# A planner's rule for blocks sent over GpSimd: which buffer the test for a free one looks at, in an induced-attention and feed-forward kernel

## The chip, the core and the metric

The kernel runs on one core of a Trainium2 chip. The metric is the device time of one execution in microseconds (us); of the kernel before it is the median of three runs. The engines are PE (TensorE, the matrix multiplier), DVE (VectorE), ACT (ScalarE), POOL (GpSimd) and SP, which issues most transfers. PEld is PE's loading of weights.

## What is computed

```python
def _attn_ref(x, inducing):                # x: 4 x 12480 x 128, inducing: 32 x 128
    def mab(q, kv):
        s = scale * (q @ kv.transpose(0, 2, 1))
        s = s - s.max(-1, keepdims=True)
        a = np.exp(s)
        a /= a.sum(-1, keepdims=True) + 1e-09
        return a @ kv
    h = mab(I, x)                          # 32 rows for each of the 4 batches
    return mab(x, h)
def _moe_ref(x, w_in, w_out):              # w_in: 128 x 2048, w_out: 2048 x 128
    h = x @ w_in
    g = np.maximum(0.01 * h, h)
    return g @ w_out
```

Each batch is read twice: a first pass makes the 32 rows h, a second lets every token attend to them, and the result goes through a feed-forward layer with a leaky activation.

## The kernel before

**Tiles.** The 49,920 tokens are cut into about 98 tiles of 512 (`tiles`; two are made of remainders and have 384). The 2048 hidden features are NF = 16 blocks of 128. A tile and a block (t, f) make one unit of work: a first product (the folded weights `hw` by the attention rows A, three quarter matmuls of 32 rows), an activation, a split of the activated block into a high part `ghi` and a low part `glo`, and second products that add w_hi·ghi, w_lo·ghi and w_hi·glo to the tile's output. The 0.01 part is linear and goes through a small matrix of its own.

**The two ways of a split.** The near way: ACT writes `ghi` from the PSUM bank (L1078, `high`), DVE writes `glo` from the same bank and `ghi` (L1081, `low`); the bank comes free after DVE. The far way: ACT writes the whole activated block to a buffer `g` (L1078 too), the bank comes free at once, and POOL makes `ghi` (a cast, L1352) and `glo` (a subtraction, L1354) from `g`. There are two buffers `g`, used in turn. In the first two tiles the same far way stands at L1050 to L1059.

**The first two tiles** (`rounds`, QUICK = 2). PE runs whole 128-row second products (L1122) in an order written out by hand. `split_first` chooses the way. `others(u)` is called after each of the 32 units u and advances the background work by a step each: conversion of the weights (`late`, whose last add on POOL is L225, with the split into w_hi and w_lo at L276 and L278), scores and values of the next batch, stores, `stacking`, and `seconds`, the second attention (`second`: scores L388, maximum L875, subtraction L879, exponent L887, sum L893, scaling L901, transpose L912). For the first group of the first batch `second` is told to use DVE in place of POOL.

**The rest** is laid out by a list planner (`turn_over`) that keeps a clock for each engine, takes the work that can start first, and emits it; the engines then run what was emitted in that order. PE runs as four row groups of 32 rows (`quarter`, L1091), a block's second products in all four, and up to GB = 10 blocks are under way. When a first product is done, `relu(i, ...)` decides between the two ways by these lines:

```python
left = far_ends[-2] if len(far_ends) > 1 else 0.0
wanted = now[0] + (i - turn_of[0]) * SLOT - EARLY
if far_open[0] < 2 and left <= start and far <= wanted:
```

`start` is when ACT could begin, `far_ends` the planned ends on POOL of the blocks whose POOL work is already laid out, `far_open` the number handed over whose POOL work is not yet laid out. After a tile's last block, ACT copies two of its four partial sums (L1380), DVE adds the other two (L1386), POOL joins them (L1397) and DVE transposes the result for the store (L1145). Work that doesn't run in four row groups, which is the scores (L388), maxima (L422), values (L559) and a few small products, waits until the planner gathers it (`clustered`), and then interrupts the quarter matmuls. `first_scores` lets group n of the next batch begin no earlier than n · PACE after that batch's begin, by the planner's clock.

Of the kernel before, what the change touches and what calls it, by code (L numbers as in the profile page):

```python
# [19 lines left out]
def induced_attention_then_leaky_ffn(  # L20
# [20 lines left out]
    nc = tc.nc  # L41
# [4 lines left out]
    NF = DFF // P  # L46
# [21 lines left out]
    PE, ACT, DVE, POOL, SP = "PE", "ACT", "DVE", "POOL", "SP"  # L68
# [14 lines left out]
    QUICK = 2  # L83
# [6 lines left out]
    SIGNAL, TO_ARRAY, TO_POOL = 35.0, 55.0, 70.0  # L90
# [3 lines left out]
    RELU, LOW, COPIED, ADDED, BLOCKS = 599.0, 690.0, 587.0, 691.0, 702.0  # L94
    FAR_HIGH, FAR_LOW, FAR_SUM = 613.0, 1297.0, 1297.0
    EARLY, PREFER, YIELDING, PATIENCE = 250.0, 0.0, 200.0, 6000.0
    IDLE, HURRY, APART, TAIL, WAITING, SOON = 600.0, 3000.0, 60000.0, 5000.0, 3000.0, 3000.0
    NEAR, BANKS, AT_ONCE, BEHIND = 3, 1, 2000.0, 1200.0
    LINEAR = NF - 3
    BEGUN = 3  # L100
    AHEAD = 100.0
    PACE, STOCK = 37000.0, 4
    debt = [0]

    const = ctx.enter_context(tc.tile_pool(name="const", bufs=1))
# [27 lines left out]
    clock = {ACT: 0.0, DVE: 0.0, POOL: 0.0, SP: 0.0}  # L133
# [4 lines left out]
    def spent(engine, ns, *after):  # L138
        if not timing[0]:
            return 0.0  # L140
        signal = TO_POOL if engine == POOL else SIGNAL
        clock[engine] = max([clock[engine], now[0], *(a + signal for a in after)]) + ns
        return clock[engine]
# [15 lines left out]
    def new(engine, at=0.0):  # L159
        if quads[0]:  # L160
            yield engine, at

    def until(test, engine=None):
        while not test():
            yield (engine, now[0] + 300.0) if quads[0] else None

    def aux_ps(name):
        return bank("aux")
# [681 lines left out]
    def second(b, g, eng=None):  # L850
        eng = eng or nc.gpsimd
        assert coming[0] == (b, g)
        yield from until(lambda: g == RG or sum(q != RG for _, q in aT) < (STOCK if quads[0] else 4))
        if (b, g) != (0, 0):
            yield from new(PE, landed.get((b, "h"), 0.0))
        hT = hw[b][0]
        _, J, K = GROUPS[g]
        rows_, w = 32 * J, 32 * K
        sp = aux_ps("s2_ps")
        for j in range(J):  # L860
            columns_product(sp, hT[:, :M], b, g, j)
        at = on_array("c", 875.0 if g != RG else 120.0, landed.get((b, "h"), 0.0), taken[0])
        del xT[b, g]
        coming.pop(0)
        ring.discard((b, g))
        yield from new(DVE, at)
        y = sb.tile([P, 16, M], F32, tag="y", name="y", bufs=1)
        yv = y[:rows_, :K, :]
        nc.vector.transpose(yv.rearrange("p k m -> p (k m)"), sp[:rows_, :w])
        at = spent(DVE, BLOCKS, at)  # L870
        done(sp, at)
        yield from old(HEAVY)
        yield from new(DVE, at)
        mx = sb.tile([P, 16], F32, tag="mx", name="mx")
        nc.vector.tensor_reduce(out=mx[:rows_, :K], in_=yv, op=ALU.max, axis=AX.X)  # L875
        at = spent(DVE, 680.0, at)
        yield from old(HEAVY)
        yield from new(POOL, at)
        eng.tensor_tensor(  # L879
            out=yv, in0=yv, in1=mx[:rows_, :K].unsqueeze(2).broadcast_to([rows_, K, M]),  # L880
            op=ALU.subtract,
        )
        at = spent(POOL, 1050.0, at)
        yield from old()
        yield from old()
        yield from new(ACT, at)
        nc.scalar.activation(yv, yv, AF.Exp, scale=SCALE)  # L887
        at = spent(ACT, 635.0, at)
        yield from old()
        yield from new(DVE, at)  # L890
        sm = sb.tile([P, 16], F32, tag="sm", name="sm")
        smv = sm[:rows_, :K]
        nc.vector.tensor_reduce(out=smv, in_=yv, op=ALU.add, axis=AX.X)  # L893
        at = spent(DVE, 680.0, at)
        yield from new(DVE, at)
        nc.vector.tensor_scalar_add(smv, smv, 1e-9)
        nc.vector.reciprocal(smv, smv)
        at = spent(DVE, 430.0)
        yield from old(HEAVY)
        yield from new(POOL, at)  # L900
        eng.tensor_tensor(  # L901
            out=yv, in0=yv, in1=smv.unsqueeze(2).broadcast_to([rows_, K, M]), op=ALU.mult
        )
        at = spent(POOL, 1050.0, at)
        yield from old()
        yield from old()
        yield from new(DVE, at)
        if g == RG:
            t = sb.tile([P, w], F32, tag="aTr", name="aTr", bufs=2)
        else:  # L910
            t = sb.tile([P, w], F32, tag="aT", name="aT", bufs=4)
        nc.vector.transpose(t[:rows_, :], yv.rearrange("p k m -> p (k m)"))  # L912
        aT[b, g] = t
        landed[b, g, "aT"] = spent(DVE, BLOCKS, at)
        yield from old(HEAVY)
# [122 lines left out]
        (t, f0) for f0 in range(0, NF, TURN) for t in range(QUICK)  # L1038
    ]

    high_of, low_of = {}, {}

    def split_first(ph, t, f, at):

        _, n = spans(t)
        ghi = sb.tile([P, TOK], F32R, tag="ghi", name="ghi", bufs=GB)
        glo = sb.tile([P, TOK], F32R, tag="glo", name="glo", bufs=GB)
        live[t, f] = (ghi, glo)
        if max(clock[POOL], at + RELU) + FAR_HIGH + FAR_LOW < max(clock[DVE], at + RELU) + LOW + BEHIND:
            g = sb.tile([P, TOK], F32, tag="g", name="g", bufs=2)  # L1050
            high(ph, g, n)
            at = spent(ACT, RELU, at)
            done(ph, at)
            nc.gpsimd.tensor_copy(ghi[:, :n], g[:, :n])
            high_of[t, f] = spent(POOL, FAR_HIGH, at)
            nc.gpsimd.tensor_tensor(  # L1056
                out=glo[:, :n], in0=g[:, :n], in1=ghi[:, :n].bitcast(F32), op=ALU.subtract
            )
            low_of[t, f] = spent(POOL, FAR_LOW)  # L1059
            return  # L1060
        high(ph, ghi, n)
        high_of[t, f] = at = spent(ACT, RELU, at)
        low(ph, ghi, glo, n)
        low_of[t, f] = at = spent(DVE, LOW, at)
        done(ph, at)
# [143 lines left out]
    with tc.manual_schedule():  # L1209
# [40 lines left out]
        def others(u):  # L1250
            debt[0] = max(0, debt[0] - 1)
            if u % 2 == 0:
                step(late)
            step(splits)
            step(weights)
            step(linear)
            if not debt[0] or u < (QUICK + 1) * NF:
                step(stores)
            step(stacking)
            if u % 2 or u < NF - 4 if u < QUICK * NF else not debt[0]:  # L1260
                step(seconds)
            if u >= due[0] and not debt[0]:
                due[0] = u + 2
                step(scores)
            if (u >= due[1] or any(b not in known for b in hw)) and not debt[0]:
                due[1] = u + 2
                if values and not (linear or weights):
                    step(values)
            follow()
# [14 lines left out]
        u = 0  # L1284
        for i, (t, f0) in enumerate(rounds):
            if 0 < i < len(rounds) - 1:
                first_round(*rounds[i + 1])
            for f in range(f0, f0 + TURN):
# [10 lines left out]
                if f == NF - 1:  # L1299
                    at = linear_part(t)  # L1300
# [24 lines left out]
        for t, parts in enumerate(tiles):  # L1325
            for b, g, _ in parts:
                tile_of.setdefault((b, g), t)
        far_ends, far_open, gathering, gang = [], [0], [0], []

        def add(engine, ready, ns, emit, allowed=None, ahead=0.0):  # L1330
            jobs[engine].append((ready, ns, emit, allowed, ahead))
# [4 lines left out]
        def relu(i, ph, ready):  # L1336
            t, f = work[i]
            _, n = spans(t)
            ghi, glo = live[t, f]
            start = max(clock[ACT], ready + SIGNAL)  # L1340
            far = max(clock[POOL], start + RELU) + backlog(POOL) + FAR_HIGH + FAR_LOW
            left = far_ends[-2] if len(far_ends) > 1 else 0.0
            wanted = now[0] + (i - turn_of[0]) * SLOT - EARLY
            if far_open[0] < 2 and left <= start and far <= wanted:
                g = sb.tile([P, TOK], F32, tag="g", name="g", bufs=2)
                high(ph, g, n)
                at = spent(ACT, RELU, ready)
                done(ph, at)
                far_open[0] += 1

                def on_pool():
                    nc.gpsimd.tensor_copy(ghi[:, :n], g[:, :n])  # L1352
                    high_at[i] = spent(POOL, FAR_HIGH, at)
                    nc.gpsimd.tensor_tensor(  # L1354
                        out=glo[:, :n], in0=g[:, :n], in1=ghi[:, :n].bitcast(F32), op=ALU.subtract
                    )
                    low_at[i] = spent(POOL, FAR_LOW)
                    far_ends.append(low_at[i])
                    far_open[0] -= 1

                add(POOL, at, FAR_HIGH + FAR_LOW, on_pool)
                return
            high(ph, ghi, n)
            high_at[i] = at = spent(ACT, RELU, ready)

            def rest():
                low(ph, ghi, glo, n)
                low_at[i] = spent(DVE, LOW, at)
                done(ph, low_at[i])

            add(DVE, at, LOW, rest)
# [240 lines left out]
        t = NT - 1  # L1612
# [48 lines left out]
```

## Time and profile before

| what | value |
|---|---|
| median of the runs | 1562.48 us (1561.61 to 1563.14, 3 runs) |
| the profiled execution | 1562.13 us |
| its span, from first to last instruction | 1560.3 us |
| PE busy | 1542.2 us (99%) |
| POOL busy | 1369.8 us (88%) |
| ACT busy | 1070.8 us (69%) |
| DVE busy | 1020.9 us (65%) |
| mean DMA rate | 82 GB/s |

The profiled execution is 1.8 us longer than its span, and 0.35 us under the median. A busy PE is not a PE at its peak: its matmuls overlap, so the time lost on it is seen in the number of matmuls in a stretch, and in the idle time before weight loads.

### The profile page before, as it was taken

What the parts mean: (1) busy time and instruction counts of PE and PEld (TensorE: products, weight loads), DVE (VectorE), ACT (ScalarE), POOL (GpSimd) and SP (SyncE); (2) the same over time, 40 slices, a digit from 0 to 9 for tenths busy, and PEclk for the clock granted to TensorE, in tenths of its full rate; (3) what the DMA queues carried; (4) which work ended last, traced back from release to release, by engine and by line L of the source; (5) the groups of instructions that cost most, each with busy time, mean ns of one, the idle gap of its engine ahead of it and who ended that gap; (6) DMA issues with size and microseconds to landing.
All of it is one profiled execution on the core that took longest, in us unless ns stands there. A gap on an engine that the chain in (4) does not pass through costs nothing.

```text
span 1560.3 us, 60204 instructions
## 1 busy us (share of the span) xinstructions
PE 1542.2 (99%) x25045; PEld 1353.0 (87%) x25045; DVE 1020.9 (65%) x1809; ACT 1070.8 (69%) x1956; POOL 1369.8 (88%) x1439
## 2 busy tenths in 40 slices
PE   8999999999999999999999999999999999999998
PEld 5578898888888798999998898989988998998896
DVE  7866667656766775666777675665565656575654
ACT  6566666666766676677676676777777777777774
POOL 1589999999999799899978989989999899959997
PEclk9999999999999999999999999999999999999999
DMA  7166454444455432354446433322222223223221
GB/s 273 17 134 110 102 104 95 97 85 93 84 107 112 99 62 66 81 100 91 92 92 131 103 76 68 63 57 56 57 56 58 55 57 63 47 55 63 55 56 24
DMA packets 400705, 128.50 MB, mean 82 GB/s; under 512 B 373136, under 2 KB 375600, under 8 KB 400432
## 3 DMA queue, kind: packets, MB, share of 16 engines
q1 hardware_dynamic: 399328, 124.50, 38.5%
q8 instruction: 197, 3.23, 0.9%
q14 instruction: 76, 0.62, 0.1%
q10 hardware_dynamic: 1104, 0.15, 0.1%
HBM read 48.94 MB, written 25.56 MB: 48 GB/s over the span
## 4 chain that ended last, share of the span: by engine, by line
PE 91%; POOL 4%; issue 2%; ACT 1%; DVE 1%; DMA 1%; SPq 1%; POOLq 0%; ACTq 0%; DVEq 0%
PE bank L1091 83%; PE bank L388 3%; POOL glo L1354 2%; PE bank L559 2%; PE bank L1122 1%; POOL ghi L1352 1%; DMA xr<-in_x_dram 1%; PE bank L708 1%; DVE glo L1081 0%; PE bank L422 0%; ACT ghi L1078 0%; SPq L373 0%; ACT g L1078 0%; POOL glo L1056 0%; PE bank L1132 0%
## 5 line engine op out<-in xcount | busy, mean ns | idle before, releaser
L1091 PE MATMUL bank<-ghi,w_hi 32*128 32x512 f32 (+1 forms) x6080 | 1251.4, 392 | 1.3 <-ACT g L1078 1.1
L1091 PE MATMUL bank<-glo,w_hi 32*128 32x512 f32 (+1 forms) x6080 | 1250.6, 391 | 0.1
L1091 PE MATMUL bank<-ghi,w_lo 32*128 32x512 f32 (+1 forms) x6080 | 1248.3, 390 | 0.0
L1091 PE MATMUL bank<-A,hwhi 32*128 32x512 f32 (+1 forms) x3394 | 1052.2, 389 | 1.6 <-DVE glo L1081 0.6
L1081 DVE SCALAR_TENSOR_TENSOR glo<-bank,ghi 128x512 fp32r<-128x512 f32 (+1 forms) x946 | 630.9, 683 | 367.5 <-ACT ghi L1078 351.2
L1091 PEld LDWEIGHTS bank<-ghi,w_hi 32*128 32x128 f32 x6080 | 822.5, 183 | 37.6 <-ACT g L1078 7.4
L1091 PEld LDWEIGHTS bank<-glo,w_hi 32*128 32x128 f32 x6080 | 825.6, 183 | 25.1 <-POOL glo L1354 1.4
L1091 PEld LDWEIGHTS bank<-ghi,w_lo 32*128 32x128 f32 x6080 | 822.7, 183 | 24.7 <-issue 3.9
L1354 POOL TENSOR_TENSOR glo<-g,ghi 128x512 fp32r<-128x512 f32 (+1 forms) x611 | 790.0, 1293 | 48.9
L1078 ACT ACTIVATE ghi<-bank 128x512 fp32r<-128x512 f32 (+1 forms) x946 | 553.7, 598 | 138.8 <-PE bank L1091 116.1
L1091 PE MATMUL bank<-A,hwlo 32*128 32x512 f32 (+1 forms) x1697 | 612.0, 386 | 0.0
L1091 PEld LDWEIGHTS bank<-A,hwhi 32*128 32x128 f32 x3394 | 568.4, 183 | 31.5 <-DVE glo L1081 5.9
L1078 ACT ACTIVATE g<-bank 128x512 f32<-128x512 f32 (+1 forms) x622 | 371.9, 598 | 275.1 <-PE bank L1091 166.4
L1352 POOL CAST ghi<-g 128x512 fp32r<-128x512 f32 (+1 forms) x611 | 374.9, 614 | 44.6 <-ACT g L1078 35.7
L1091 PEld LDWEIGHTS bank<-A,hwlo 32*128 32x128 f32 x1697 | 297.8, 183 | 5.2 <-issue 0.8
L1386 DVE TENSOR_TENSOR part<-bank,part 128x512 f32<-128x512 f32 (+1 forms) x190 | 129.8, 686 | 97.6 <-ACT part L1380 47.8
L1397 POOL TENSOR_TENSOR part<-part 128x512 f32<-128x512 f32 (+1 forms) x95 | 122.7, 1292 | 15.8 <-DVE part L1386 15.7
L1380 ACT COPY part<-bank 128x512 f32<-128x512 f32 (+1 forms) x190 | 110.6, 587 | 15.0 <-PE bank L1091 12.3
L1145 DVE STREAM_TRANSPOSE osb<-part 128x512 f32<-128x512 f32 (+1 forms) x95 | 66.5, 700 | 9.0 <-POOL part L1397 7.7
L515 DVE STREAM_TRANSPOSE xT<-xc 128x512 f32<-128x512 f32 x72 | 46.4, 683 | 0.0
L448 ACT ACTIVATE e<-e,nm 128x512 f32<-128x512 f32 (+1 forms) x28 | 18.7, 669 | 24.6 <-DVE least L436 21.4
L879 POOL TENSOR_TENSOR y<-y,mx 128x512 f32<-128x512 f32 (+1 forms) x27 | 25.4, 941 | 9.0 <-DVE mx L875 8.6
(122 smaller groups left out, 658.3 us busy)
## 6 DMA issues: line engine op xcount, KB each, us to landing
A<-both SPq DMA_DIRECT2D x376, 128.0 KB, 2.4
xr<-in_x_dram SPq DMA_DIRECT2D x96, 256.0 KB, 4.8
out_dram<-osb SPq DMA_DIRECT2D x382, 64.0 KB, 2.2
xc<-in_x_dram SPq DMA_DIRECT2D x288, 64.0 KB, 2.8
raw<-in_moe_w_in_dram SPq DMA_DIRECT2D x4, 512.0 KB, 6.6
raw<-in_moe_w_out_dram SPq DMA_DIRECT2D x4, 512.0 KB, 8.4
A<-both SPq DMA_DIRECT2D x48, 16.0 KB, 1.8
out_dram<-osb SPq DMA_DIRECT2D x48, 8.0 KB, 1.8
```

What stands on the lines that cost most here:

```text
L388: nc.tensor.matmul(dst, lhsT, rhs, start=True, stop=True)
L515: nc.vector.transpose(t[:, j, :], blk.rearrange("p n c -> p (n c)"))
L559: nc.tensor.matmul(hp[32 * k : 32 * k + 32, :C], ay[:rows_, 4 * q + k, :], xb[:rows_, k, :], start=(q == 0), stop=(4 * q + 4 >= K), tile_p ...
L1078: nc.scalar.activation(ghi[:, :n], ph[:, :n], AF.Relu)
L1081: nc.vector.scalar_tensor_tensor(out=glo[:, :n], in0=ph[:, :n], scalar=0.0, in1=ghi[:, :n].bitcast(F32), op0=ALU.max, op1=ALU.subtract,)
L1091: nc.tensor.matmul(dst, w[32 * r : 32 * r + 32], x[32 * r : 32 * r + 32], start=start, stop=stop, tile_position=(32 * r, 0),)
L1145: nc.vector.transpose(osb[:, :n], total[:, :n])
L1352: nc.gpsimd.tensor_copy(ghi[:, :n], g[:, :n])
L1354: nc.gpsimd.tensor_tensor(out=glo[:, :n], in0=g[:, :n], in1=ghi[:, :n].bitcast(F32), op=ALU.subtract)
L1380: nc.scalar.copy(part[:, :n], po[:, :n])
L1386: nc.vector.tensor_tensor(out=part[:, :n], in0=po[:, :n], in1=part[:, :n], op=ALU.add)
L1397: nc.gpsimd.tensor_tensor(out=total[:, :n], in0=total[:, :n], in1=part[:, :n], op=ALU.add)
```

## The change

It alters five places of the planner; no operation on data is changed.

```diff
-    PACE, STOCK = 37000.0, 4
+    PACE, STOCK = 39000.0, 4
...
-        at = spent(POOL, 1050.0, at)
+        at = spent(*((POOL, 1050.0) if eng is nc.gpsimd else (DVE, 690.0)), at)
...
-        at = spent(POOL, 1050.0, at)
+        at = spent(*((POOL, 1050.0) if eng is nc.gpsimd else (DVE, 690.0)), at)
...
-    high_of, low_of = {}, {}
+    high_of, low_of, far_ends = {}, {}, []
...
-        if max(clock[POOL], at + RELU) + FAR_HIGH + FAR_LOW < max(clock[DVE], at + RELU) + LOW + BEHIND:
+        start = max(clock[ACT], at + SIGNAL)
+        if far_ends[-2:-1] <= [start] and max(clock[POOL], start + RELU) + FAR_HIGH + FAR_LOW < (
+            max(clock[DVE], start + RELU) + LOW + BEHIND
+        ):
...
             low_of[t, f] = spent(POOL, FAR_LOW)
+            far_ends.append(low_of[t, f])
             return
...
-            if u % 2 or u < NF - 4 if u < QUICK * NF else not debt[0]:
+            if u % 2 or u < NF + 4 if u < QUICK * NF else not debt[0]:
                 step(seconds)
...
-        far_ends, far_open, gathering, gang = [], [0], [0], []
+        far_open, gathering, gang = [0], [0], []
...
-            left = far_ends[-2] if len(far_ends) > 1 else 0.0
+            left = far_ends[far_open[0] - 2] if far_open[0] < 2 <= len(far_ends) + far_open[0] else 0.0
```

In `relu`, with one block handed over and not yet laid out, the next `g` is the buffer of the last block laid out, so the test now looks at `far_ends[-1]`, where it looked at `far_ends[-2]`. `split_first` gets a test for a free `g`, and counts from ACT's clock. `second` books the two steps that run on DVE on DVE's clock. `seconds` is advanced at every unit up to u = 19 (it was 11) and at every other one after. PACE goes from 37 to 39 us.

The number of instructions hardly changes: PE has 24,324 matmuls in both programs, and three blocks of 512 columns go from the far way to the near (613 to 610 far, 923 to 926 near, the 384-column ones the same). Their order changes from the middle of the first two tiles to the end. Three places follow; line numbers of the change are 4 higher than before from the relu rule on (L1078 is L1082, L1091 is L1095, L1380 is L1384), and 3 higher in `split_first` (L1054 is L1057, L1056 is L1059).

ACT, at the end of a tile some 456 us into the trace, around the eighth copy of attention rows (`both`); `g` is a block that goes over POOL. Before:

```order
L1078 ACTIVATE g<-bank_67 128x512
L1078 ACTIVATE ghi<-bank_70 128x512
L1078 ACTIVATE g<-bank_65 128x512
L1078 ACTIVATE ghi<-bank_71 128x512
L1078 ACTIVATE g<-bank_67 128x512
L1078 ACTIVATE ghi<-bank_65 128x512
L1078 ACTIVATE g<-bank_70 128x512
L932 CAST both<-aT 128x512
L1380 COPY part<-bank_66 128x512
L1380 COPY part<-bank_64 128x512
```

and now:

```order
L1082 ACTIVATE ghi<-bank_71 128x512
L1082 ACTIVATE ghi<-bank_67 128x512
L1082 ACTIVATE g<-bank_65 128x512
L448 ACTIVATE e,zg<-e,nm 128x512
L455 ACTIVATE al<-nm 128x1
L1082 ACTIVATE g<-bank_71 128x512
L1384 COPY part<-bank_69 128x512
L932 CAST both<-aT 128x512
L1082 ACTIVATE ghi<-bank_65 128x512
L1384 COPY part<-bank_70 128x512
```

Four blocks in seven went to `g` ahead of the copies, with the copies behind them; now two do in the same stretch, and the copies stand among the blocks.

PE, in the first pass over batch 2, around the values of one group (`ay`) and the scores of others (`xT`); each run of rows other than L1091 ends the four row groups for a while. Before, four such runs some 100 rows or fewer apart:

```order
L1091 MATMUL bank_64<-ghi,w_lo 128x512
L422 MATMUL bank_66<-rd,e_74 128x4
L1091 MATMUL bank_65<-ghi,w_hi 128x512
...
L388 MATMUL bank_71<-xT,hT 32x512 x4
...
L388 MATMUL bank_67<-xT,indT 32x512 x4
...
L559 MATMUL bank_65<-xr,ay 32x128 x16
```

and now, at the place nearest to it:

```order
L1095 MATMUL bank_65<-A_9771,hwhi 128x512
L388 MATMUL bank_66<-xT,hT 32x512 x4
L388 MATMUL bank_69<-xT,indT 32x512 x4
L422 MATMUL bank_64<-rd,e_74 128x4
L559 MATMUL bank_66<-xr,ay 32x128 x16
L1095 MATMUL bank_70<-glo,w_hi 128x512
```

The same work stands in one run. Between the first two tiles and the last one, 42 such runs are left of 46.

POOL, at the end of the first two tiles: the last conversion of weights (L225), the split of the last w_out quarter (L278, `w_lo`), and the second attention (`y`). Before:

```order
L225 TENSOR_TENSOR wraw<-cv_a,cv_t 128x512
L879 TENSOR_TENSOR y<-y,mx 128x512
L278 TENSOR_TENSOR w_lo<-wraw,w_hi 128x512
L1054 CAST ghi<-g 128x512
L1056 TENSOR_TENSOR glo<-g,ghi 128x512
L901 TENSOR_TENSOR y<-y,sm 128x512
```

and now:

```order
L225 TENSOR_TENSOR wraw<-cv_a,cv_t 128x512
L901 TENSOR_TENSOR y<-y,sm 128x512
L1057 CAST ghi<-g 128x512
L1059 TENSOR_TENSOR glo<-g,ghi 128x512
L278 TENSOR_TENSOR w_lo<-wraw,w_hi 128x512
L1057 CAST ghi<-g 128x512
```

The subtraction L879 went ahead of L225, and a scaling and a whole far block went ahead of L278.

## Rows read from the trace of the kernel before

**Rows 1.** The page: busy time of the engines, and PE's granted clock by slices.

```profile
PE 1542.2 (99%) x25045; PEld 1353.0 (87%) x25045; DVE 1020.9 (65%) x1809; ACT 1070.8 (69%) x1956; POOL 1369.8 (88%) x1439
...
PEclk9999999999999999999999999999999999999999
```

**Rows 2.** Windows, quarter matmuls alone (L1091): length, PE busy (count), PEld busy (count), clock, DMA.

```profile
90.00:530.00 440.00, 406.42 (x6654) 358.23 (x6657) 1.00 0.51 102
530.00:960.00 430.00, 400.43 (x6814) 368.77 (x6810) 1.00 0.44 89
960.00:1541.00 581.00, 572.93 (x9750) 528.30 (x9742) 1.00 0.27 55
```

**Rows 3.** Timeline: two whole second products after each other; start, length, instruction.

```profile
76.44 0.39 PE L1122 MATMUL bank<-ghi,w_lo 128*128 128x512 f32 x1
...
76.67 0.40 PE L1122 MATMUL bank<-glo,w_hi 128*128 128x512 f32 x1
```

**Rows 4.** Waits of PE's weight loads, 90 to 1541 us: total us, times, longest.

```profile
PEld bank L1091 <- ACT g L1078: 9.6, 26, 0.9
PEld bank L1091 <- issue: 8.4, 23, 0.8
PEld bank L1091 <- DVE glo L1081: 6.7, 14, 0.8
...
PEld bank L1091 <- ACT part L1380: 5.1, 18, 0.7
```

**Rows 5.** Waits of ACT, whole span.

```profile
ACT g L1078 <- PE bank L1091: 166.4, 300, 4.6
...
ACT g L1078 <- POOL glo L1354: 84.7, 142, 1.7
```

**Rows 6.** Timeline around 455 us: POOL, ACT and PE's weight loads; in brackets idle before, and its end.

```profile
452.70 1.29 POOL L1354 TENSOR_TENSOR glo<-g,ghi 128x512 fp32r<-128x512 f32 x1
454.03 0.60 ACT L1078 ACTIVATE g<-bank 128x512 f32<-128x512 f32 x1 [0.84 <-POOL glo L1354]
454.63 1.29 POOL L1354 TENSOR_TENSOR glo<-g,ghi 128x512 fp32r<-128x512 f32 x1
455.96 0.60 ACT L1078 ACTIVATE g<-bank 128x512 f32<-128x512 f32 x1 [0.84 <-POOL glo L1354]
456.45 0.61 ACT L932 CAST both<-aT 128x512 fp32r<-128x512 f32 x1
456.61 0.18 PEld L1091 LDWEIGHTS bank<-ghi,w_hi 32*128 32x128 f32 x2 [0.64 <-ACT g L1078]
456.96 0.59 ACT L1380 COPY part<-bank 128x512 f32<-128x512 f32 x1
```

**Rows 7.** The tile glo, whole span: count, duration ns min/median/max, first and last start, forms.

```profile
L1081 DVE SCALAR_TENSOR_TENSOR glo<-bank,ghi x946: 547/691/694, 46.0 to 1549.7; 128x512 fp32r<-128x512 f32 x185, 128x384 fp32r<-128x384 f32 x5
L1354 POOL TENSOR_TENSOR glo<-g,ghi x611: 1007/1297/1317, 94.6 to 1544.1; 128x512 fp32r<-128x512 f32 x151, 128x384 fp32r<-128x384 f32 x2
```

**Rows 8.** Timeline, end of the first two tiles: PE's wait for L225, POOL, first use of w_lo.

```profile
67.82 1.16 PE L339 MATMUL bank<-wraw,winT 128*128 128x128 f32 x8 [1.06 <-POOL wraw L225]
76.78 1.29 POOL L225 TENSOR_TENSOR wraw<-cv_a,cv_t 128x512 f32<-128x512 f32 x1 [1.55 <-DVE cv_t L220]
78.02 1.06 POOL L879 TENSOR_TENSOR y<-y,mx 128x512 f32<-128x512 f32 x1
79.03 1.29 POOL L278 TENSOR_TENSOR w_lo<-wraw,w_hi 128x512 fp32r<-128x512 f32 x1
81.14 0.19 PEld L1122 LDWEIGHTS bank<-ghi,w_lo 128*128 128x128 f32 x1
83.03 1.29 POOL L1056 TENSOR_TENSOR glo<-g,ghi 128x512 fp32r<-128x512 f32 x1
```

**Rows 9.** Timeline of PE's weight loads at two of the runs that interrupt L1091.

```profile
507.55 0.30 PEld L422 LDWEIGHTS bank<-rd,e 128*128 128x128 f32 x2 [0.37 <-issue]
...
514.11 0.16 PEld L388 LDWEIGHTS bank<-xT,hT 128*32 128x32 f32 x8 [0.36 <-issue]
```

## The prediction

> **What bounds the kernel now.** I read the page of the profile first: PE is busy 99% of the span and POOL 88% [rows 1]; the granted clock is 1.00 in all three stretches of the windows [rows 2]. So the clock plays no part, and what can be gained is time in which PE is "busy" with fewer matmuls than it could run. For that I read the windows of the quarter matmuls alone. Two second products in a row start 0.23 us apart [rows 3], and four row groups work side by side, so a quarter matmul of 512 columns costs 0.23 / 4 = 0.058 us. The three stretches of the planned part hold 6654, 6814 and 9750 of them in 406.4, 400.4 and 572.9 us [rows 2]; at 0.058 us each that would be 385.9, 395.2 and 565.5. So at least 20.5 + 5.2 + 7.4 = 33 us are lost between quarter matmuls, most of it in the first third; it is more than that, since some matmuls are narrower.
>
> The waits of PE's weight loads say where this goes: for ACT's writing of a `g` 9.6 us in 26 waits, for DVE's `glo` 6.7 in 14, for ACT's copies of partial sums 5.1 in 18, and 8.4 us in which the profile shows no releaser [rows 4]. No transfer is among the large rows. The next question is what ACT itself waited for before it wrote those `g`: 166.4 us for PE, which is work not there yet and harmless, and 84.7 us, in 142 waits, for POOL's `glo`, which is a `g` buffer not yet free [rows 5]. Such a wait is 0.60 us in the mean, and because an engine's work is taken in the order laid out, everything behind it on ACT waits too. The timeline around 455 us shows one that reaches PE: POOL's subtraction begins at 452.70 and 454.63, each time ACT has stood 0.84 us for the buffer that it frees, the second `g` begins at 455.96, and PE's next load, which needs the bank that this `g` empties, comes at 456.61 after 0.64 us idle. The copy of a partial sum, due there as well, begins only at 456.96 [rows 6].
>
> The planner did not see these waits: with one block handed over and not laid out, it looked at the wrong one of the two buffers.
>
> **The change, part by part.**
>
> *The relu rule.* A block for which no `g` is free when ACT could start takes the near way. Nearly as many blocks go far as before (610 of 613), so POOL keeps its load and the three extra near blocks cost DVE 3 x 0.69 us [rows 7] on an engine that is busy 65% [rows 1]: nothing, and if that cover were gone, 2 us. What changes is when. ACT's waits for POOL should nearly go. Not quite: the planner books a far block at 613 + 1297 = 1910 ns, and the two subtractions start 1.93 us apart [rows 6], so behind ten far blocks in a row POOL is some 0.2 us later than planned, a third of the mean wait of 0.60. I therefore take two thirds of PE's wait for `g`, 9.6 x 2/3 = 6.4 us gained; bounds are nothing and all 9.6. The waits for `glo` and for copies, 6.7 + 5.1 = 11.8 us, are in part of the same origin, as the copy at 456.96 is, and in part the ordinary crowd at the end of a tile, where two copies, two sums and a join fall due together. I take a sixth, 2.0 us, nearer to the lower end, since the rows name ACT and DVE as busy there and only the example shows the buffer behind them; bounds are nothing and half, 5.9.
>
> *Fewer interruptions.* Before a run of other matmuls PE's loads stand idle 0.36 to 0.37 us [rows 9], where 0.06 would be usual, so a run costs 0.31 us beside its own work. Four runs fewer (42 for 46) give 4 x 0.31 = 1.2 us. Below, this is bounded by nothing, if the merged runs start later than what waits for them can bear; above by twice that, if the row groups also lose time in starting again.
>
> *Seconds at every unit up to u = 19, the first tiles' rule, and DVE's own price.* Here the program is short enough to follow. A scores product now runs ahead of the wait for L225 at 67.82, which was 1.06 us [rows 8], and would cover most of it; but the next L225, at 76.78, still waits for the same conversion on DVE, and takes that gain back. Behind it POOL now has a scaling and a whole far block ahead of the split into w_lo. L225 ends at 78.07; a scaling is taken at L879's 1.06, a far block at 1.93 and the split at 1.29 [rows 6, 8]. That puts w_lo at 78.07 + 1.06 + 1.93 + 1.29 = 82.35, and PE's first load of it was at 81.14 [rows 8]. PE's order there is as it was, so it waits 1.2 us more. The bounds are a gain of 1.1 (the wait at 67.82 covered and kept) and a loss of 1.9 (PE there earlier by the rest of that cover). What the scores product does in the first tiles it no longer does in the planned part, so its own time is moved and not added. Attention rows come a little earlier, and nothing waits for them in the rows.
>
> *PACE.* Group n of a next batch's scores begins n x 2 us later, 12 us for the last. A batch lasts about a quarter of 1560 us, 390 us, and seven groups at 39 us take 273, so some 100 us of slack hide it; without that slack it would be up to 12 us for each of three batches. Transfers for these groups move with them on SP's queue; I price that at nothing for the same reason.
>
> Sum: -6.4 - 2.0 - 1.2 + 1.2 = -8.4 us. The profiled execution took 1562.13 us, so 1553.7; the median lies 0.35 us higher, so the forecast is **1554 us**. Its own range is 1546 (all 9.6 of the first term, half of the second, the interruptions, the early part even) to 1558.
>
> **The rivals.**
>
> *The wait changes its name.* PE stands at a tile's end because ACT, DVE and POOL all have the sums to make there; a refused block goes to DVE and its bank is free just as late. Near, a bank is held for 0.60 + 0.69 = 1.29 us [rows 6, 7]; far with a mean wait, 0.60 + 0.60 = 1.20. Then the first two terms are nil, and 1562.5 - 1.2 + 1.2 = 1562.5 us is left. For it speaks how close those two sums are; against it, that with the wait gone the near blocks and copies behind it on ACT are no longer held up, as two instructions were in the example [rows 6]. One more way to the same end would be that DVE's `glo` stands still while POOL works. Of 946 such instructions on DVE the longest took 694 ns against a median of 691, beside a POOL busy 88% [rows 1, 7], so it does not happen here. The Trainium skill (Perfetto Trace Analysis, Optimizing Scalar/DVE Operations) warns that the two engines share an SBUF read port, so that moving work between them might not help; by that rule the gain would be nil, and by the row it is as summed. Chance 0.19.
>
> *Slower: banks.* A near block holds its bank until DVE has made its `glo`, and at a tile's end DVE also has two sums, so a refused block there can hold its bank for 1.29 + 0.69 us and more. A wait of PE for `glo` is 6.7 / 14 = 0.48 us [rows 4]. The forecast's gain is gone once 8.4 / 0.48 = 18 refused blocks, one tile in five, meet a sum in that way. At one tile in three, 33 x 0.48 = 15.7 us, it is 1562.5 - 8.4 + 15.7 = 1570 us. Against it: DVE is idle a third of the time [rows 1], and the new order puts fewer far blocks ahead of the copies. The Trainium skill (TensorEngine Tiling (Array Packing), Restrictions and Gotchas) states that row tiling adds to the pressure on PSUM, since row tiles write to different banks; no row here shows the rule itself. Chance 0.12.
>
> *It does not do what it says.* If POOL's lag behind the planner is larger than 0.2 us where it counts, half of the waits stay: -3.2 - 1.0 - 1.2 + 1.2 = -4.2, 1558.3 us. Chance 0.10.
>
> Besides, the whole order is drawn anew from the first tiles on, so waits that have nothing to do with `g` move as well. The rows that could change so, 8.4 and 11.8 us [rows 4], let me allow 4 us to both sides, which is within the ranges given.
>
> **The numbers.** Forecast 0.59, half of it 0.10, changed name 0.19, banks 0.12. A measurement of this kernel can tell some 0.2% from no change, 3.1 us: the first two cases are faster, the third the same, the last slower, so 0.69, 0.19 and 0.12. The range takes in the first three cases, 1546 to 1563 us, and leaves out the fourth and a little below.
>
> **What would show it.** In the changed profile ACT's wait for POOL's `glo` should be under 30 us in under 80 waits (was 84.7 in 142), PE's wait for `g` near 3 us, and the stretch from 90 to 530 us should show the most added matmuls per microsecond. POOL's busy time should stay within 1%. Around 82 us the first loads of w_lo should come after a wait for POOL. The forecast is wrong if ACT still waits over 50 us for POOL, if PE's waits for `glo` grow past 12 us, which is the banks' case, or if the sum of PE's waits stays at 30 us under other names.

## The result and the profile after

The changed kernel takes 1546.07 us in the median (1545.6 to 1546.52, 4 runs), beside 1562.05 (1561.4 to 1563.14) for the kernel before on the same chip: a ratio of 0.9897 [0.988, 0.9914]. That is 16.0 us gained where 8.4 were forecast. The direction and the mechanism were as predicted, the size was about twice the forecast, and the time lies at the very low end of the range. The profiled execution took 1546.52 us, with a span of 1544.7.

The page of the changed kernel, its busy times and its chain by engine:

```profile
PE 1529.6 (99%) x25045; PEld 1364.2 (88%) x25045; DVE 1032.5 (67%) x1812; ACT 1081.2 (70%) x1956; POOL 1362.4 (88%) x1433
...
PE 96%; DVE 1%; ACT 1%; POOL 1%; DMA 1%; issue 0%; SPq 0%; ACTq 0%; POOLq 0%
```

POOL is as busy as before to within 0.6%, and ACT and DVE are a little busier in a shorter span [rows 1]. The chain of work that ended last, followed back from the last instruction, now runs over PE for 96%; before it was 91%, with 4% on POOL:

```profile
PE 91%; POOL 4%; issue 2%; ACT 1%; DVE 1%; DMA 1%; SPq 1%; POOLq 0%; ACTq 0%; DVEq 0%
```

The windows of the quarter matmuls (columns as in rows 2, which the first two answer to; the third ends at 1525 us here, since the changed kernel ends earlier):

```profile
90.00:530.00 440.00, 406.67 (x6817) 368.35 (x6820) 1.00 0.50 99
530.00:960.00 430.00, 402.19 (x6869) 371.44 (x6861) 1.00 0.45 93
960.00:1525.00 565.00, 556.04 (x9535) 525.39 (x9536) 1.00 0.28 57
```

Over the first 440 us, 163 more matmuls were run, over the next 430 us 55 more, at the same granted clock of 1.00 [rows 2]. In the third stretch, cut at 1525 us in both traces, it is 9535 against 9498; before:

```profile
960.00:1525.00 565.00, 556.93 (x9498) 515.43 (x9493) 1.00 0.28 56
```

The waits of PE's weight loads, from 90 to 1525 us:

```profile
PEld bank L388 <- issue: 10.3, 32, 0.4
PEld bank L1095 <- issue: 7.3, 23, 0.8
...
PEld bank L1095 <- POOL glo L1358: 3.0, 11, 0.5
...
PEld bank L1095 <- DVE glo L1085: 1.7, 5, 0.8
...
PEld bank L1095 <- ACT g L1082: 1.6, 7, 0.3
...
PEld bank L1095 <- ACT part L1384: 0.9, 5, 0.2
```

[Rows 4] go up to 1541 us, which is about as far from the end of the longer program. Against them, the wait for `g` fell from 9.6 to 1.6 us, the one for DVE's `glo` from 6.7 to 1.7, the one for ACT's copies from 5.1 to 0.9. From 90 to 1525 us in both traces, all rows of this view for quarter matmuls together came to 33.3 us before and 16.4 now; all rows for other loads to 43.3 and 43.2.

What ACT waits for before it writes a `g`, whole span:

```profile
ACT g L1082 <- PE bank L1095: 174.3, 337, 3.6
...
ACT g L1082 <- POOL glo L1358: 24.3, 51, 1.3
ACT g L1082 <- POOL ghi L1356: 20.8, 44, 1.7
```

The wait for POOL's `glo` was 84.7 us in 142 waits [rows 5]. The one for POOL's `ghi` was 11.9 us in 23 waits, and has grown, so that the two together went from 96.6 to 45.1. Before:

```profile
ACT g L1078 <- POOL ghi L1352: 11.9, 23, 1.6
```

### The profile page after: what moved, and what is told of

The parts are those of the page before. It is cut to its first block, busy times and chain, and to the rows that moved or that the text cites. A ratio compares the mean times of both kernels' runs of the same rounds, so it can differ in the third digit from the quotient of the medians.

```text
span 1544.7 us, 60217 instructions
## 1 busy us (share of the span) xinstructions
PE 1529.6 (99%) x25045; PEld 1364.2 (88%) x25045; DVE 1032.5 (67%) x1812; ACT 1081.2 (70%) x1956; POOL 1362.4 (88%) x1433
## 4 chain that ended last, share of the span: by engine, by line
PE 96%; DVE 1%; ACT 1%; POOL 1%; DMA 1%; issue 0%; SPq 0%; ACTq 0%; POOLq 0%
PE bank L1095 88%; PE bank L388 3%; PE bank L1126 2%; PE bank L559 2%; PE bank L708 1%; DMA xr<-in_x_dram 1%; PE bank L422 1%; DVE glo L1085 0%; POOL glo L1358 0%; ACT xT L714 0%; ACT ghi L1082 0%; PE bank L1136 0%; PE bank L803 0%; ACT g L1082 0%; PE bank L1001 0%
## 5 line engine op out<-in xcount | busy, mean ns | idle before, releaser
L1095 PE MATMUL bank<-ghi,w_hi 32*128 32x512 f32 (+1 forms) x6080 | 1213.4, 391 | 0.0
L1095 PE MATMUL bank<-glo,w_hi 32*128 32x512 f32 (+1 forms) x6080 | 1210.2, 390 | 0.1
L1095 PE MATMUL bank<-ghi,w_lo 32*128 32x512 f32 (+1 forms) x6080 | 1209.8, 390 | 0.0
L1095 PE MATMUL bank<-A,hwhi 32*128 32x512 f32 (+1 forms) x3394 | 1042.9, 388 | 0.1
L1095 PEld LDWEIGHTS bank<-ghi,w_hi 32*128 32x128 f32 x6080 | 787.9, 183 | 25.5 <-issue 1.2
L1095 PEld LDWEIGHTS bank<-ghi,w_lo 32*128 32x128 f32 x6080 | 789.3, 183 | 21.9 <-issue 2.9
L1095 PEld LDWEIGHTS bank<-glo,w_hi 32*128 32x128 f32 x6080 | 787.4, 183 | 23.9 <-POOL glo L1358 3.0
L1082 ACT ACTIVATE ghi<-bank 128x512 fp32r<-128x512 f32 (+1 forms) x949 | 556.9, 597 | 151.5 <-PE bank L1095 122.2
L1095 PE MATMUL bank<-A,hwlo 32*128 32x512 f32 (+1 forms) x1697 | 615.5, 386 | 0.0
L1095 PEld LDWEIGHTS bank<-A,hwhi 32*128 32x128 f32 x3394 | 563.2, 183 | 20.7 <-DVE glo L1085 2.4
L1082 ACT ACTIVATE g<-bank 128x512 f32<-128x512 f32 (+1 forms) x619 | 370.3, 598 | 228.3 <-PE bank L1095 174.3
L1095 PEld LDWEIGHTS bank<-A,hwlo 32*128 32x128 f32 x1697 | 298.5, 183 | 4.9 <-issue 0.2
L1384 ACT COPY part<-bank 128x512 f32<-128x512 f32 (+1 forms) x190 | 110.8, 584 | 17.0 <-PE bank L1095 14.5
L939 POOL TENSOR_TENSOR both<-aT,both 128x512 fp32r<-128x512 f32 x24 | 31.8, 1325 | 0.0
```

The source lines that it names most:

```text
L939: (eng or nc.gpsimd).tensor_tensor(out=alo[sl], in0=aT.pop((b, g))[: 32 * J, :], in1=ahi[sl].bitcast(F32), op=ALU.subtract,)
L1082: nc.scalar.activation(ghi[:, :n], ph[:, :n], AF.Relu)
L1095: nc.tensor.matmul(dst, w[32 * r : 32 * r + 32], x[32 * r : 32 * r + 32], start=start, stop=stop, tile_position=(32 * r, 0),)
L1384: nc.scalar.copy(part[:, :n], po[:, :n])
```

## The experiments

**Theory A**: ACT standing for a `g` buffer is what PE lost its time to, directly and through all that is queued on ACT behind it. **The rivals** look for the gain elsewhere: in the newly drawn order of the blocks as such (theory B in the expectations), or in the other parts of the change, which are PACE and the first two tiles (theory C). Each run stands beside the kernel before on its own chip, whose median was 1563.09 to 1563.18 us. The last column is ACT's wait for POOL's `glo` ahead of a `g`, read from each run's waits as above.

| label | edit | median us (range) | ratio to before | ACT's wait, us in times |
|---|---|---|---|---|
| e4_pace39 | before + PACE 39 | 1575.07 (1574.13 to 1575.76) | 1.0075 [1.0063, 1.0088] | 123.8 in 178 |
| e3_control | before, XR 6 | 1562.81 (1561.42 to 1563.07) | 0.9996 [0.9987, 1.0005] | 89.7 in 148 |
| e2_old_relu | changed, old relu test | 1560.42 (1559.17 to 1561.54) | 0.9981 [0.9972, 0.9989] | 75.0 in 111 |
| e5_first_tiles | changed, old relu test, PACE 37 | 1563.97 (1562.84 to 1565.17) | 1.0006 [0.9997, 1.0015] | 72.1 in 114 |
| e6_pace37 | changed, PACE 37 | 1548.33 (1547.9 to 1549.44) | 0.9906 [0.9892, 0.992] | 28.1 in 58 |
| e1_relu_rule | before + new relu test | 1547.03 (1546.32 to 1547.9) | 0.9895 [0.9882, 0.9909] | 21.1 in 45 |
| e3_three_g | before, 3 buffers g, XR 6 | 1548.72 (1548.64 to 1550.33) | 0.9908 [0.9895, 0.9922] | 15.8 in 30 |
| e7_three_g_after | changed, 3 buffers g, XR 6 | 1546.69 (1546.41 to 1547.02) | 0.9894 [0.9881, 0.9908] | 13.8 in 34 |
| e10_three_g_rule | the same, tests count 3 | 1548.96 (1547.87 to 1549.36) | 0.9908 [0.9894, 0.9921] | 11.1 in 23 |
| e8_pool_booked | changed, far block booked longer | 1545.87 (1544.63 to 1546.76) | 0.9889 [0.9874, 0.9904] | 2.9 in 11 |

### One part of the change alone

The new test in `relu`, and nothing else:

```diff
-            left = far_ends[-2] if len(far_ends) > 1 else 0.0
+            left = far_ends[far_open[0] - 2] if far_open[0] < 2 <= len(far_ends) + far_open[0] else 0.0
```

> The kernel before with the relu rule alone (the test looks at the buffer that is reused); PACE, the first two tiles and DVE's booking as before. Theory A, the buffer: the gain comes from ACT no longer standing for a g buffer. Then most of the 16 us is here: 1546 to 1550 us, ACT's wait for POOL's glo near 25 us in 50 waits, PE's waits for g, glo and copies together near 5 us (21.4 before, 4.2 after). Theory B, the redrawn order: any edit of the planner gives another order, and this one was lucky. Then this kernel lies anywhere between 1550 and 1566 us with ACT's wait just as low. Theory C, the other parts of the change: 1558 to 1563 us.

It gains 1.05%, as much as the whole change. The rest of the change is not needed for the gain. It draws the order anew too, so it doesn't decide between A and B.

The changed kernel with the same line put back:

```diff
-            left = far_ends[far_open[0] - 2] if far_open[0] < 2 <= len(far_ends) + far_open[0] else 0.0
+            left = far_ends[-2] if len(far_ends) > 1 else 0.0
```

> The changed kernel with the old test in relu, all other parts of the change kept. Theory A: the gain is gone, 1558 to 1564 us, with ACT's wait for POOL's glo back over 60 us. Theory B: anywhere between 1546 and 1566 us. Theory C: 1546 to 1550 us although ACT's wait is back.

Of the gain of 1.03% only 0.19% is left, and the waits are back: ACT 75.0 us in 111, and PE's 8.7 us for `g`, 5.8 for `glo`, 3.8 for copies, near [rows 4]. The waits of ACT and of PE's quarter loads in that run:

```profile
ACT g L1082 <- POOL glo L1358: 75.0, 111, 2.1
```

```profile
PEld bank L1095 <- ACT g L1082: 8.7, 26, 1.2
...
PEld bank L1095 <- DVE glo L1085: 5.8, 13, 0.8
PEld bank L1095 <- ACT part L1384: 3.8, 12, 0.6
```

The first-tile parts alone are this kernel with PACE at its old value too:

```diff
-    PACE, STOCK = 39000.0, 4
+    PACE, STOCK = 37000.0, 4
...
-            left = far_ends[far_open[0] - 2] if far_open[0] < 2 <= len(far_ends) + far_open[0] else 0.0
+            left = far_ends[-2] if len(far_ends) > 1 else 0.0
```

> The kernel before with the first two tiles' parts of the change alone (the test for a free g there, DVE's own price, seconds at every unit up to u = 19); the old test in relu and PACE 37 us. Theory A (only ACT's wait for g counts, and the early part costs about 1 us): ACT's wait for POOL's glo stays over 70 us and the time within 1558 to 1566 us; from the second L339 to the end of the first two tiles 1 to 2 us longer than before. Theory C (these parts bring some of the gain): 1550 to 1557 us.

No difference to before: 1.0006 [0.9997, 1.0015]. The stretch named in the expectation took 30.4 us, where it was 28.5, as expected. This run also settles whether the gain could come from sending fewer blocks over POOL: it sends 37 fewer than the kernel before (574 subtractions for 611), the change only 3 fewer, and nothing is gained.

```profile
L1358 POOL TENSOR_TENSOR glo<-g,ghi x574: 1015/1298/1316, 95.4 to 1544.0; 128x512 fp32r<-128x512 f32 x191, 128x384 fp32r<-128x384 f32 x1
```

PACE alone on the kernel before, and PACE put back in the changed kernel:

```diff
-    PACE, STOCK = 37000.0, 4
+    PACE, STOCK = 39000.0, 4
```

> The kernel before with PACE at 39 us alone; the old test in relu, the first two tiles as before. It has 50 interruptions of the quarter matmuls where the kernel before has 46. Theory A (only ACT's wait for g counts): ACT's wait for POOL's glo stays over 70 us and the time within 1559 to 1567 us; 4 interruptions at 0.31 us would be 1.2 us more. If a longer pace by itself spreads the work better: under 1558 us.

```diff
-    PACE, STOCK = 39000.0, 4
+    PACE, STOCK = 37000.0, 4
```

> The changed kernel with PACE back at 37 us. Theory A: 1544 to 1550 us, ACT's wait for POOL's glo under 30 us; the order is another one, so the spread against the changed kernel shows what drawing the order anew is worth. If PACE carries the gain: over 1553 us.

The first of the two was a miss: 1575.07 us, 12 us slower than before and far outside what was expected. Its ACT waits and PE's three large waits:

```profile
ACT g L1078 <- POOL glo L1354: 123.8, 178, 2.7
```

```profile
PEld bank L1091 <- ACT g L1078: 15.1, 35, 1.1
...
PEld bank L1091 <- DVE glo L1081: 7.8, 19, 0.8
...
PEld bank L1091 <- ACT part L1380: 4.5, 20, 0.5
```

ACT stands 39 us longer for a buffer than in [rows 5], in 178 waits for 142. From 90 to 1525 us all waits of quarter loads came to 40.3 us (33.3 before) and those of other loads to 45.9 (43.3), so 9.6 of the 12 us stand there. This fits the same mechanism with the opposite sign: PACE draws the whole order anew, and under the old test the order that came out collided more often. It is not shown, since no run gave this order a third buffer, and it also sends 16 blocks more over POOL and interrupts the quarter matmuls 50 times for 46. With the new test the same 2 us of PACE are worth some 0.1% (e6 against the changed kernel, ratios 0.9906 and 0.9897 with intervals that overlap), and with the old test and the new first tiles PACE 39 is even 3.5 us faster than 37 (e2 against e5). So PACE has no fixed price here; it depends on the order that it leads to.

### A third buffer, the order unchanged

The cleanest test of A leaves every instruction where it was and only takes away what ACT waits for. A third `g` needs room, which comes from one buffer fewer for the loads of x (XR); the planner lays out the same instructions in the same order as in the kernel before.

```diff
-    XR = 7
+    XR = 6
...
-            g = sb.tile([P, TOK], F32, tag="g", name="g", bufs=2)
+            g = sb.tile([P, TOK], F32, tag="g", name="g", bufs=3)
...
-                g = sb.tile([P, TOK], F32, tag="g", name="g", bufs=2)
+                g = sb.tile([P, TOK], F32, tag="g", name="g", bufs=3)
```

> The kernel before with a third buffer g and, to make room for it, six buffers for rows of x in place of seven. The planner's rules are untouched, and every engine runs the same instructions in the same order as in the kernel before. Theory A: ACT's 84.7 us of waits for POOL's glo go to under 10 us, PE's waits for g, glo and copies from 21.4 us to under 8, and the time falls by 10 to 16 us, to 1546 to 1552 us. Theory B or C: the order is the same, so ACT's waits go but the time stays within 1557 to 1562 us.

Its control gives up the buffer of XR and nothing else:

```diff
-    XR = 7
+    XR = 6
```

> The kernel before with six buffers for rows of x in place of seven and two buffers g, same order: the price of the room that the third g takes. All theories: 1561 to 1566 us, since a load of rows may start later, and nothing else differs.

The control is as fast as the kernel before (0.9996 [0.9987, 1.0005]), and the third buffer alone gives 0.9908 [0.9895, 0.9922], which is 14.4 of the 16 us. No block changed its way, no load was moved, PACE and the first tiles are the old ones. Of the whole change, this is the part that a free `g` explains, and theory B falls with it. ACT's wait fell less far than was expected (to 15.8 us, where under 10 was written). ACT's waits, whole span, and those of PE's quarter loads, 90 to 1525 us:

```profile
ACT g L1078 <- POOL glo L1354: 15.8, 30, 2.5
ACT g L1078 <- POOL ghi L1352: 14.1, 33, 1.6
```

```profile
PEld bank L1091 <- issue: 7.4, 21, 0.8
...
PEld bank L1091 <- POOL glo L1354: 4.0, 16, 0.5
...
PEld bank L1091 <- DVE glo L1081: 2.9, 6, 0.8
...
PEld bank L1091 <- ACT part L1380: 1.9, 11, 0.2
...
PEld bank L1091 <- ACT g L1078: 1.0, 4, 0.3
```

The wait for `g` lost 8.6 us against [rows 4], the one for DVE's `glo` 3.8, the one for copies 3.2. DVE and the copies had nothing changed but the moment at which ACT came to them. The place of [rows 6] can be followed in this trace, since the instructions are the same; here is ACT around 450 us, from the first `g` of that group of four:

```profile
446.64 0.59 ACT L1078 ACTIVATE g<-bank 128x512 f32<-128x512 f32 x1
447.12 0.59 ACT L1078 ACTIVATE ghi<-bank 128x512 fp32r<-128x512 f32 x1
447.80 0.60 ACT L1078 ACTIVATE g<-bank 128x512 f32<-128x512 f32 x1
448.50 0.60 ACT L1078 ACTIVATE ghi<-bank 128x512 fp32r<-128x512 f32 x1
449.86 0.60 ACT L1078 ACTIVATE g<-bank 128x512 f32<-128x512 f32 x1 [0.76 <-PE bank L1091]
450.49 0.60 ACT L1078 ACTIVATE ghi<-bank 128x512 fp32r<-128x512 f32 x1
451.28 0.60 ACT L1078 ACTIVATE g<-bank 128x512 f32<-128x512 f32 x1 [0.19 <-POOL ghi L1352]
451.78 0.61 ACT L932 CAST both<-aT 128x512 fp32r<-128x512 f32 x1
452.29 0.59 ACT L1380 COPY part<-bank 128x512 f32<-128x512 f32 x1
```

The four `g` are those at 450.51, 452.10, 454.03 and 455.96 in the trace of before. From the first of them to the copy took 456.96 - 450.51 = 6.45 us there, with waits of 0.52, 0.84 and 0.84 us for POOL in it, and takes 452.29 - 446.64 = 5.65 here. One of the waits is now for PE, which is work that is not there yet. PE's load that had stood 0.64 us for the last of these `g` has no wait here.

### Is there more to be had?

If A holds, the waits that the changed kernel still has could be worth a quarter us each, or nothing. Three kernels took them away in different ways: a third buffer in the changed kernel with its order unchanged,

```diff
-    XR = 7
+    XR = 6
...
-            g = sb.tile([P, TOK], F32, tag="g", name="g", bufs=2)
+            g = sb.tile([P, TOK], F32, tag="g", name="g", bufs=3)
...
-                g = sb.tile([P, TOK], F32, tag="g", name="g", bufs=2)
+                g = sb.tile([P, TOK], F32, tag="g", name="g", bufs=3)
```

> The changed kernel, same order on every engine, with a third buffer g and six buffers for rows of x. It takes away what is left of ACT's wait (24.3 us for POOL's glo). Theory A with the price found so far, 14 us for some 69 us of such waits: 20 us of waits less, 1 to 4 us faster, 1542 to 1545 us. If the rest of these waits falls where nobody needs ACT: 1545 to 1548 us.

the time at which the planner books POOL's two steps, raised by 20 ns for a block,

```diff
-    FAR_HIGH, FAR_LOW, FAR_SUM = 613.0, 1297.0, 1297.0
+    FAR_HIGH, FAR_LOW, FAR_SUM = 628.0, 1302.0, 1297.0
```

> The changed kernel with a far block booked on POOL at 628 + 1302 = 1930 ns, as the trace has it, in place of 1910, so that POOL does not fall behind the plan. Theory A with the rest of the waits free of charge (as with three buffers on the changed order): ACT's wait for POOL's glo falls under 15 us and the time stays at 1544 to 1550 us. If POOL's lag behind the plan is what the change left on the table: 1540 to 1544 us.

and the third buffer with tests that count on it, so that the order changes too (beside the edits of e7_three_g_after):

```diff
-        if far_ends[-2:-1] <= [start] and max(clock[POOL], start + RELU) + FAR_HIGH + FAR_LOW < (
+        if far_ends[-3:-2] <= [start] and max(clock[POOL], start + RELU) + FAR_HIGH + FAR_LOW < (
...
-            left = far_ends[far_open[0] - 2] if far_open[0] < 2 <= len(far_ends) + far_open[0] else 0.0
+            left = far_ends[far_open[0] - 3] if far_open[0] < 3 <= len(far_ends) + far_open[0] else 0.0
...
-            if far_open[0] < 2 and left <= start and far <= wanted:
+            if far_open[0] < 3 and left <= start and far <= wanted:
```

> The changed kernel with three buffers g and the planner's tests counting three (in relu and in the first two tiles), six buffers for rows of x. Up to two blocks can wait for POOL without ACT waiting. Theory A: ACT's waits under 15 us, 1541 to 1547 us, POOL's load as before. If POOL, always fed, is what limits then: PE's waits for POOL's glo grow past 8 us and the time is 1547 to 1555 us.

None is faster than the changed kernel beyond the uncertainty of the comparison (0.9894, 0.9889 and 0.9908, beside its 0.9897). The first two came out by the readings in which the rest of the wait is free. The third was a miss: 1548.96 us is slower than theory A had it, and the sign of the other reading isn't there either, since PE's wait for POOL's `glo` is 2.2 us and not over 8. In e8_pool_booked ACT's wait for `glo` is all but gone:

```profile
ACT g L1082 <- POOL ghi L1356: 16.2, 37, 0.9
...
ACT g L1082 <- POOL glo L1358: 2.9, 11, 0.6
```

It fell by 21.4 us against the changed kernel, and the time did not follow. That agrees with the lag that the prediction had seen, from subtractions 1.93 us apart against 1.91 booked, but doesn't show it: with the longer booking the planner also sends 21 blocks fewer over POOL (587 subtractions for 608), in another order. The cleaner case is e7_three_g_after, where the order is the changed kernel's: 10.5 us of the wait are gone there, and no time with them.

Over all ten runs the time follows ACT's wait, roughly, down to some 25 us and no further. Between e1 and e4, (1575.07 - 1547.03) / (123.8 - 21.1) = 0.27 us of the kernel for each us of the wait; between 21 and 3 us of wait the times scatter from 1546 to 1549 without a trend. It is a slope between two runs and no law: e5 waits 17.6 us less than the control, and is 1.2 us slower. Theory A stands, with that floor, and its rivals fall: neither the first tiles nor PACE gives the gain, and the free buffer gives 14.4 of the 16 us without them and in the old order.

## Where the prediction was right, and the step that failed

**What bounds the kernel, and the mechanism: right.** PE's lost time between quarter matmuls, and in it the waits that begin with ACT standing for a buffer. The three signs named for it came out: ACT's wait for `glo` at 24.3 us in 51 waits (under 30 in under 80 was asked), PE's wait for `g` at 1.6 us (near 3), and the first stretch with the most added matmuls (163 in 440 us). One sign is weaker than it was put: the wait for POOL's `ghi` ahead of a `g` grew by 8.9 us. The prediction had not named that row.

**The wait for `g`, -6.4 us: a little small.** It fell by 8.0 in the changed kernel, by 8.6 with the third buffer. The third that was to stay, from POOL's 0.2 us of lag, stayed on ACT (24.3 of 84.7 us, close to a third) but hardly reached PE. The error was to carry the share from ACT's waits over to PE's: what is left on ACT falls where PE doesn't need it, as e7_three_g_after shows by removing 10.5 us of it, in the same order, for nothing.

**The work queued behind, -2.0 us: this is the step that failed.** The prediction took a sixth of 6.7 + 5.1 = 11.8 us, "since the rows name ACT and DVE as busy there and only the example shows the buffer behind them", with half as the upper bound. Measured, those two rows lost 5.0 + 4.2 = 9.2 us in the changed kernel, over three quarters, and more than that bound of 5.9. With the third buffer, the order unchanged, they lost 7.0. The 7.2 us between -2.0 and -9.2 are nearly all of the 7.6 us by which the forecast fell short; the errors of the other terms roughly cancel. So most of these waits were the same wait at one or two removes. The trace of before shows it, at 541 us; first ACT, then DVE and PE's weight load:

```profile
539.30 0.60 ACT L1078 ACTIVATE g<-bank 128x512 f32<-128x512 f32 x1 [0.84 <-POOL glo L1354]
539.79 0.59 ACT L1078 ACTIVATE ghi<-bank 128x512 fp32r<-128x512 f32 x1
540.27 0.59 ACT L1380 COPY part<-bank 128x512 f32<-128x512 f32 x1
540.74 0.63 ACT L1078 ACTIVATE ghi<-bank 128x512 fp32r<-128x512 f32 x1
...
540.42 0.69 DVE L1081 SCALAR_TENSOR_TENSOR glo<-bank,ghi 128x512 fp32r<-128x512 f32 x1 [1.17 <-ACT ghi L1078]
...
541.16 0.18 PEld L1091 LDWEIGHTS bank<-A,hwhi 32*128 32x128 f32 x1 [0.68 <-DVE glo L1081]
```

PE's 0.68 us are booked to DVE. But DVE had just stood 1.17 us for ACT's `ghi`, and ACT had written that `ghi` right after the `g` for which it stood 0.84 us. DVE was late, not busy. Of the 14 waits for `glo` in [rows 4], 12 have the end of such a stop of ACT within them or in the 4 us before, of the 18 for copies 16, of the 26 for `g` 23. Of the 23 loads without a releaser it is 3. The 4 us behind the 142 stops cover 31% of the time from 90 to 1541 us, so this is no accident of a crowded trace. That count could have been made before the change; the prediction looked at one example, and let the name of the releaser, the last link, stand for the cause.

**Waits that came in exchange.** PE's wait for POOL's `glo` rose from 1.4 us to 3.0, and to 4.0 with the third buffer; its loads without a releaser went from 8.4 to 7.3. With the rows above, -8.0 - 5.0 - 4.2 + 1.6 - 1.1 = -16.7 us, and all quarter loads together 33.3 - 16.4 = 16.9 less. Waits of loads are not time lost one for one, though: in e5_first_tiles quarter loads wait 29.9 us and others 42.2, which is 4.5 less than before, and it is no faster. That the sum below closes so well is in part luck.

**Fewer interruptions, -1.2 us: not seen.** The waits ahead of the scores products, where the profile shows no releaser, went from 11.2 us in 34 to 10.3 in 32; but all waits of loads other than the quarter ones stayed at 43.3 and 43.2 us. No run isolated this term, so its size stays open; in the sum it is nothing. The third buffer gave its gain with all 46 interruptions, and e8_pool_booked has 47 and is as fast as the changed kernel with 42, so it is not what the gain rests on.

**The early part, +1.2 us: right.** POOL's order and PE's first load of w_lo in the changed kernel:

```profile
77.96 1.29 POOL L225 TENSOR_TENSOR wraw<-cv_a,cv_t 128x512 f32<-128x512 f32 x1 [0.63 <-DVE cv_t L220]
79.72 1.05 POOL L901 TENSOR_TENSOR y<-y,sm 128x512 f32<-128x512 f32 x1 [0.46 <-DVE sm L897]
...
81.40 1.27 POOL L1059 TENSOR_TENSOR glo<-g,ghi 128x512 fp32r<-128x512 f32 x1
82.64 1.26 POOL L278 TENSOR_TENSOR w_lo<-wraw,w_hi 128x512 fp32r<-128x512 f32 x1
```

```profile
83.95 0.19 PEld L1126 LDWEIGHTS bank<-ghi,w_lo 128*128 128x128 f32 x1 [0.88 <-POOL w_lo L278]
```

The scaling and a far block stand ahead of the split, and PE waits for POOL as named. From the end of L225 to that of the split are 82.64 + 1.26 - 77.96 - 1.29 = 4.65 us, where 4.28 were summed from single durations. The stretch from the second use of wraw to the last whole second products of these tiles took 1.8 us longer than before. The scores products in it (L388) kept PE busy for 2.13 us where it was 1.38, and that work was only moved there, so the loss is some 1.1 us. Absolute times can't be compared: the first L339 comes at 55.40 us in the kernel before and at 56.95 in e1_relu_rule, which is the same program up to there. With the loss, the sum is -16.7 + 1.1 = -15.6 us, and 16.0 were measured.

**PACE and three blocks moved to DVE, nothing: right for the change as a whole**, but to price PACE at nothing because some 100 us of slack hide it was right for a wrong reason. In e4_pace39 the groups were moved by the same 2 us each and the time rose by 12 us, most likely through the order.

**The rivals.** That the wait changes its name falls: the quarter loads' waits were halved, and nothing took their place but the 1.6 us on POOL. The rule weighed there (the Trainium skill, Perfetto Trace Analysis, Optimizing Scalar/DVE Operations), that moving work between DVE and GpSimd might not help because of a shared port, does not bind here; three blocks more on DVE, and its longest `glo` is still 694 ns, at a median of 692:

```profile
L1085 DVE SCALAR_TENSOR_TENSOR glo<-bank,ghi x949: 517/692/694, 47.5 to 1534.1; 128x512 fp32r<-128x512 f32 x186, 128x384 fp32r<-128x384 f32 x4
```

The rival of the banks falls as well: PE's wait for DVE's `glo`, which would have passed 12 us, fell to 1.7 (its price of 33 x 0.48 us is 15.8, not 15.7, which changes nothing). That half of the waits stay falls with ACT's 24.3 us.

## What to carry to other kernels

A wait on an engine that works in order is priced with everything behind it: for each wait of the bounding engine, follow its releaser one or two steps further back, and count how many end at the same stop, before taking a share. A planner's test for a free buffer must look at the buffer that will be reused, and count blocks handed over but not yet laid out; whether such a stop costs anything is best tested by one buffer more with the order unchanged. And an edit that only redraws an order (PACE here) has no price of its own: under the old test it moved the time by -3.5 us in one kernel and by +12 in another, under the new one by 0.1%, which is within the uncertainty.

## What had not been expected

That ACT's stops have a floor below which they are free: between 123.8 and 21 us each us of the wait was worth 0.27 us in the mean, and from there to 2.9 nothing that ten runs could tell. Of PE's remaining 16.4 us of waits ahead of quarter loads the largest row, 7.3 us, has no releaser in the profile, and no run was made to find it.
